# Part A's input transposed by DMA in natural token order, and read by the products with a token step of 16

## The chip, the cores and the metric

One core of a Trainium2 chip. The metric is the device time of one execution in microseconds (us); lower is better. Single executions of this kernel vary by some per cent on some chips (the kernel before took 177.28 and 177.91 us in its first rounds, 177.11 to 183.49 in those of e1), so each run carries a state (slow: more than 1.5% above the fastest run of the same kernel in its rounds; unknown: a single run), and only fast runs are compared.

In the profile, PE is TensorE's matmul stream, PEld its weight loads, DVE is VectorE, ACT is ScalarE, POOL is GpSimd, SP is the engine that issues most DMAs. The granted clock (PEclk) is the TensorE clock that the profile shows as granted, as a share of full speed. "L496" is a line of the kernel's file. The line numbers shift a little from kernel to kernel: the products that this study turns on are L496 before, L486 after, and between L486 and L498 in the experiments. They all write `u_ps`.

## The reference, cut to what matters

Part A is a linear recurrence over 2048 tokens; part B (local attention) has its own inputs and shares only the engines.

```python
dt = exp(log_dt);  Lam_bar = exp(dt * Lam)                 # complex, 448 states
Bu = einsum("bld,pd->blp", x, ((Lam_bar - 1) / Lam)[:, None] * Bmat)
h_t = Lam_bar * h_(t-1) + Bu_t                             # 2048 steps
y = 2 * einsum("blp,dp->bld", h, Cmat).real + x * Dskip
```

## The kernel before

Tokens are split into 128 chunks of 16: token = 16 p + j, with j = 4 a + b. `local(b)` computes B x for the tokens of one b, in products with 512 columns (4 values of a, 128 chunks), and adds the step from b-1. The products read x with its features on the partitions, so this kernel has TensorE transpose it, and ScalarE stores it with the 512 columns of each b side by side.

```python
def load_x(self):                       # natural rows, one DMA for each half
    self.x_sb = self.pool.tile([NCH, T, D], bf16, name="xa_sb", tag="xin")
    ...
def alloc(self):
    xa = pool.tile([KP, 4, KT, 4, NCH], bf16, name="xaT", tag="xT")   # [112, b, k, a, chunk]
    self.xT = {i: xa[:, i] for i in range(4)}
def transp(self, b, eng):               # 16 PE transposes and 2 evictions for each b
    for a in range(0, 4, 2):
        ...
                nc.tensor.transpose(pt[:, k, i, :], self.x_sb[:, 4 * (a + i) + b, k * KP:(k + 1) * KP], cx.ident[:])
        cx.ev(eng, t_[:, :, a:a + 2, :], pt[:])
def local(self, b):
    for m in range(NM):                                     # 7 blocks of states
        for k in range(KT):                                 # 4 blocks of features
            nc.tensor.matmul(ps[:], lhsT=self.Bcat[:, k, m, :],
                             rhs=self.xT[b][:, k].rearrange("p a c -> p (a c)"), ...)
        if b % 2:  ...  # + mats[1] x h[b - 1]
        if b == 3: ...  # + mats[2] x h[1]
        nc.scalar.copy(self.h[b][:, m, :], ps[:])
```

After `local` come the scan over chunks (`scan`, products `g3A`, then VectorE), corrections (`correct`) and outputs (`y`). Part B's attention sums (`pv`, written to `pvb` and `pvt`) run on VectorE beside all this. They need `vd`, some of whose rows are copied between partitions by DMA (the halo copies). The order of instructions on each engine is fixed at build time by a scheduler, not by the order of the source.

Of the kernel before, what the change touches and what calls it, by code (L numbers as in the profile page):

```python
# [10 lines left out]
ACT = mybir.ActivationFunctionType  # L11
ALU = mybir.AluOpType
f32 = mybir.dt.float32
bf16 = mybir.dt.bfloat16

S = 2048
D = 448
T = 16
NCH = 128
KT = 4  # L20
KP = 112
# [8 lines left out]
NW = 32  # L30
NM = 7
PL = 64
MA = 4
TWO_PI = 2.0 * math.pi
MAGIC = 12582912.0
# [52 lines left out]
class PartB:  # L88
# [64 lines left out]
    def transp(self, n, eng):  # L153
        nc, cx = self.nc, self.cx
        pt = cx.ps([KP, KT, 2, NCH], bf16, "pt_x", "pt")
        for i in range(2):
            for k in range(KT):
                nc.tensor.transpose(pt[:, k, i, :], self.x_sb[:, n + i, k * KP:(k + 1) * KP], cx.ident[:])
        cx.ev(eng, self.xT[:, :, n * NCH:(n + 2) * NCH], pt[:].rearrange("p k i c -> p k (i c)"))
# [115 lines left out]
class PartA:  # L275
# [7 lines left out]
    def load_params(self):  # L283
        nc, pool = self.nc, self.pool
        self.prow = pool.tile([3 * NM, 2, PL], bf16, name="prow")
        self.drow = pool.tile([KT, KP], bf16, name="drow")
        for i, src in enumerate((self.A_logdt, self.A_Lre, self.A_Lim)):
            v = src.rearrange("(m p) -> m p", p=PL).unsqueeze(1).to_broadcast([NM, 2, PL])
            nc.scalar.dma_start(self.prow[i * NM:(i + 1) * NM], v)
        nc.scalar.dma_start(self.drow[:], self.A_Dskip.rearrange("(k p) -> k p", p=KP))  # L290

    def load_bc(self):
        nc, pool = self.nc, self.pool
# [7 lines left out]
                nc.sync.dma_start(self.cn[:, a, :, ri, :], v[:, a])  # L301

    def load_x(self):
        self.x_sb = self.pool.tile([NCH, T, D], bf16, name="xa_sb", tag="xin")
        xv = self.A_x[0].rearrange("(p j) d -> p j d", j=T)
        for g in range(2):
            self.nc.sync.dma_start(self.x_sb[:, 8 * g:8 * g + 8, :], xv[:, 8 * g:8 * g + 8, :])

    def consts(self):
        nc, pool = self.nc, self.pool  # L310
# [7 lines left out]
    def params(self):  # L318
        nc, pool, V = self.nc, self.pool, self.nc.vector
        ident = self.cx.ident  # L320

        def sm(name, shape=(NCH, NM), tag=None):
            return pool.tile(list(shape), f32, name=name, tag=tag or name)

        pt = self.cx.ps([NCH, 3 * NM], bf16, "pt_p", "lg")
# [3 lines left out]
        ll = sm("ll", (NCH, 2, NM))  # L329
        V.tensor_copy(ll[:].rearrange("p r m -> p (r m)"), pt[:, NM:3 * NM])  # L330
        lre, lim = ll[:, 0], ll[:, 1]
        ptd = self.cx.ps([KP, KT], bf16, "pt_d", "lg")
        nc.tensor.transpose(ptd[:], self.drow[:], ident[0:KT, 0:KT])
        dsk = sm("dsk", (KP, KT))
        V.tensor_copy(dsk[:], ptd[:])
        kv = pool.tile([NCH, NPW, NM], f32, name="kv")
        for i, kk in enumerate(KPOW):
# [60 lines left out]
    def params_g(self):  # L398
        nc, G, ident = self.nc, self.nc.vector, self.cx.ident
        lre, lim, rden, Scat, dsk = self.lre, self.lim, self.rden, self.Scat, self.dsk  # L400
        la_re, la_im = self.pw_re[:, 0, :], self.pw_im[:, 0, :]

        def sm(name):
            return self.pool.tile([NCH, NM], f32, name=name)

        lm1, g_re, g_im, t1 = (sm(n) for n in ("lm1", "g_re", "g_im", "t1"))
        G.tensor_scalar(lm1[:], la_re, -1.0, None, op0=ALU.add)
        G.tensor_tensor(g_re[:], lm1[:], lre, op=ALU.mult)
        G.tensor_tensor(t1[:], la_im, lim, op=ALU.mult)
        G.tensor_tensor(g_re[:], g_re[:], t1[:], op=ALU.add)  # L410
        G.tensor_tensor(g_re[:], g_re[:], rden[:], op=ALU.mult)
        G.tensor_tensor(g_im[:], la_im, lre, op=ALU.mult)
        G.tensor_tensor(t1[:], lm1[:], lim, op=ALU.mult)
        G.tensor_tensor(g_im[:], t1[:], g_im[:], op=ALU.subtract)
        G.tensor_tensor(g_im[:], g_im[:], rden[:], op=ALU.mult)
        self.mat("g", self.rot_rows("Sg", g_re, g_im)[:], G)
        self.Dg = self.pool.tile([KP, KT, KP], bf16, name="Dg")
        for k in range(KT):
            nc.scalar.activation(self.Dg[:, k, :], ident[0:KP, 0:KP], ACT.Copy, scale=dsk[:, k:k + 1])

    def params_m(self):
        for i in range(NPW):
# [21 lines left out]

    def setup_b(self, engs):
        nc, cx, pool = self.nc, self.cx, self.pool
        self.Bcat = pool.tile([KP, KT, NM, NCH], bf16, name="Bcat")
        for i in range(NM):
            pt = cx.ps([KP, KT, NCH], f32, "pt_b", "pt")
            for k in range(KT):  # L450
                nc.tensor.matmul(pt[:, k, :], lhsT=self.bX[:, i, k * KP:(k + 1) * KP], rhs=self.mats["g"][:, i, :],
                                 start=(k == 0), stop=(k == KT - 1), skip_group_check=True)
            cx.ev(engs[i % len(engs)], self.Bcat[:, :, i, :], pt[:])
            yield

    def setup_c(self, engs):
        nc, cx, pool = self.nc, self.cx, self.pool
# [9 lines left out]
            yield  # L467

    def alloc(self):
        pool = self.pool  # L470
        xa = pool.tile([KP, 4, KT, 4, NCH], bf16, name="xaT", tag="xT")
        self.xT = {i: xa[:, i] for i in range(4)}
        u01 = pool.tile([NCH, 2, NM, 4 * NCH], bf16, name="u01", tag="q")
        self.h = [u01[:, 0], u01[:, 1], None, None]

    def transp(self, b, eng):
        nc, cx = self.nc, self.cx
        t_ = self.xT[b]
        for a in range(0, 4, 2):
            pt = cx.ps([KP, KT, 2, NCH], bf16, "pt_x", "pt")  # L480
            for i in range(2):
                for k in range(KT):
                    nc.tensor.transpose(pt[:, k, i, :], self.x_sb[:, 4 * (a + i) + b, k * KP:(k + 1) * KP],
                                        cx.ident[:])
            cx.ev(eng, t_[:, :, a:a + 2, :], pt[:])
            yield  # L486

    def local(self, b):
        nc, cx = self.nc, self.cx
        if b == 2:  # L490
            u23 = self.pool.tile([NCH, 2, NM, 4 * NCH], bf16, name="u23", tag="xin")
            self.h[2], self.h[3] = u23[:, 0], u23[:, 1]
        for m in range(NM):
            ps = cx.ps([NCH, 4 * NCH], f32, "u_ps", "mm")
            for k in range(KT):
                nc.tensor.matmul(ps[:], lhsT=self.Bcat[:, k, m, :], rhs=self.xT[b][:, k].rearrange("p a c -> p (a c)"),  # L496
                                 start=(k == 0), stop=(b % 2 == 0 and k == KT - 1))
            if b % 2:  # L498
                nc.tensor.matmul(ps[:], lhsT=self.mats[1][:, m, :], rhs=self.h[b - 1][:, m, :], start=False,
                                 stop=(b == 1))  # L500
            if b == 3:
                nc.tensor.matmul(ps[:], lhsT=self.mats[2][:, m, :], rhs=self.h[1][:, m, :], start=False, stop=True)  # L502
            nc.scalar.copy(self.h[b][:, m, :], ps[:])  # L503
            yield

    def _regs(self, nm):
# [92 lines left out]
    def y(self, a, b):  # L599
        nc, cx, pool = self.nc, self.cx, self.pool  # L600
        j = 4 * a + b
        ps = cx.ps([NCH, D], f32, "y_ps", "mm")
        for k in range(KT):
            nc.tensor.matmul(ps[:, k * KP:(k + 1) * KP], lhsT=self.xT[b][:, k, a, :], rhs=self.Dg[:, k, :],  # L604
                             start=(k == 0), stop=False, skip_group_check=True)
        for m in range(NM):
            nc.tensor.matmul(ps[:], lhsT=self.state(m, a, b), rhs=self.C[:, m, :], start=False, stop=(m == NM - 1),  # L607
                             skip_group_check=True)
        ya = pool.tile([NCH, D], bf16, name="ya", tag="ya", bufs=2)
        nc.scalar.copy(ya[:], ps[:])  # L610
        nc.sync.dma_start(self.out_a[:, j, :], ya[:])
# [3 lines left out]
def body(ctx: ExitStack, tc: tile.TileContext, A_x, A_Lre, A_Lim, A_Bre, A_Bim, A_Cre, A_Cim, A_logdt, A_Dskip,  # L615
         B_x, B_wqkv, B_wo, out):
    nc = tc.nc
    pool = ctx.enter_context(tc.tile_pool(name="sb", bufs=1))
    psum = ctx.enter_context(tc.tile_pool(name="ps", bufs=1, space=bass.MemoryType.PSUM))
    out_v = out[0].rearrange("(p j) e -> p j e", j=T)  # L620
    cx = Ctx(tc, pool, psum)
    b = PartB(cx, B_x, B_wqkv, B_wo, out_v[:, :, D:2 * D])
    a = PartA(cx, A_x, A_Lre, A_Lim, A_Bre, A_Bim, A_Cre, A_Cim, A_logdt, A_Dskip, out_v[:, :, 0:D])
# [38 lines left out]
    def weave(main, fill, k=1):  # L662
        for _ in main:
            for _ in range(k):
                next(fill, None)
        for _ in fill:
            pass
# [10 lines left out]
    a.params_m()  # L678
    b.norm()
    a.alloc()  # L680
    for _ in a.transp(0, "A"):
        pass
    weave(a.local(0), chain(a.transp(1, "A"), a.transp(2, "A")))
    weave(a.local(1), chain(a.transp(3, "A"), a.setup_c("A")))
    for b_ in (2, 3):
        for _ in a.local(b_):
            pass
    a.scan()
# [3 lines left out]
    for a_ in range(4):  # L692
        a.y(a_, 3)
    for b_ in (1, 0, 2):
        for _ in a.correct(b_, "A"):
            pass
        if b_ == 1:
            b.pv(4, 8)
        if b_ == 0:
            b.pv(8, 12)  # L700
        for a_ in range(4):
            a.y(a_, b_)
# [32 lines left out]
```

## Time and profile before

| | before |
|---|---|
| time | 177.59 us, median of 2 runs (177.28 to 177.91) |
| PE / DVE / ACT busy | 91% / 76% / 62% of 175.3 us |
| `u_ps` products | 112, started 216 to 217 ns apart |
| first `u_ps` product, scan's first VectorE operation | 78.84 us, 114.78 us |

The page of the kernel before: span, busy time by engine, the span in 40 slices (busy tenths, and the granted TensorE clock in tenths), then a group of instructions (busy time, mean ns of one, idle time before them and what ended it).

```profile
span 175.3 us, 2965 instructions
PE 159.6 (91%) x1171; PEld 90.8 (52%) x1175; DVE 132.6 (76%) x189; ACT 108.9 (62%) x183; POOL 5.6 (3%) x37
...
PE   7589798799799999999999999969999999999981
DVE  1299998999996894039999999999999999900000
PEclk9999999999999999999999999999999999999999
...
L496 PE MATMUL u_ps<-xaT,Bcat 112*128 112x512 bf16 x112 | 27.4, 379 | 0.1
```

A matmul's listed duration (379 ns) is longer than its spacing (216 to 217 ns): in the profile the matmuls overlap. What a product costs the stream is the distance between starts, which the timeline gives. The timeline of PE, and one line of DVE (start us, us in all, engine, line, operation):

```profile
78.84 1.24 PE L496 MATMUL u_ps<-xaT,Bcat 112*128 112x512 bf16 x5
96.55 7.07 PE L496 MATMUL u_ps<-xaT,Bcat 112*128 112x512 bf16 x32
103.68 0.38 PE L502 MATMUL u_ps<-u,mat 128*128 128x512 bf16 x1
111.47 0.38 PE L502 MATMUL u_ps<-u,mat 128*128 128x512 bf16 x1
114.78 0.68 DVE L531 TENSOR_TENSOR pc<-g3A,cosE 128x512 bf16<-128x512 f32 x1
```

The 32 products from 96.55 to 103.68 us, with the one contiguous product of another line that the trace lacks among them, are (103.68 - 96.55) / 33 = 216 ns apart; other stretches give 217, which is used below. The last product of `local` starts at 111.47 us, and scan's VectorE work at 114.78 us.

The table of windows (each column: busy us and number of instructions; at the end the granted clock, the DMA share and GB/s) shows that PE and DVE are both full in this stage:

```profile
core 0: us, PE busy (x) PEld busy (x) DVE busy (x) ACT busy (x) POOL busy (x), PEclk, DMA share, GB/s
...
83.00:96.50 13.50, 13.39 (x101) 7.70 (x102) 13.50 (x14) 12.33 (x19) 0.00 (x0) 1.00 0.01 1
96.50:111.70 15.20, 15.14 (x71) 6.83 (x71) 15.20 (x16) 8.20 (x14) 0.00 (x0) 1.00 0.01 1
```

Weight loads by shape in the kernel before (mean ns of one after the busy time):

```profile
L177 PEld LDWEIGHTS <-xbT 112*128 112x128 bf16 x64 | 8.8, 146 | 4.0 <-issue 1.3 <-PE lg L196 0.4
L604 PEld LDWEIGHTS <-xaT 112*128 112x128 bf16 x64 | 4.7, 97 | 2.7 <-issue 0.2
...
L229 PEld LDWEIGHTS <-e_all 128*128 128x128 bf16 x16 | 1.5, 146 | 0.4
```

L177 and L229 load 128 columns that are 16 elements apart, L604 adjacent ones: 146 against 97 ns.

### The profile page before, as it was taken

To read this page: it belongs to the slowest core of one execution; us is meant where nothing else is said; L and a number is where in the kernel's file an instruction comes from. 1 tells how busy PE (TensorE), PEld (TensorE's weight loads), DVE (VectorE), ACT (ScalarE), POOL (GpSimd) and SP (SyncE) were. 2 spreads that over 40 slices of the span, in tenths; PEclk is the share of its full clock that TensorE was granted. 3 is DMA by queue.
4 is the path that set the end of the run, shared out by engine and by line. 5 is a ranking of instruction groups with operands and counts; after the bars stand their busy time and mean duration, and the time that the engine had idled before them with its cause. 6 is when DMAs were issued, how large, how long until landed. Compare 5 with 4: busy or idle time off the path is not lost.

```text
span 175.3 us, 2965 instructions
## 1 busy us (share of the span) xinstructions
PE 159.6 (91%) x1171; PEld 90.8 (52%) x1175; DVE 132.6 (76%) x189; ACT 108.9 (62%) x183; POOL 5.6 (3%) x37
## 2 busy tenths in 40 slices
PE   7589798799799999999999999969999999999981
PEld 4355333445444766676565444746755455554550
DVE  1299998999996894039999999999999999900000
ACT  2279444775744876788899654356238739738382
POOL 8400000000000000000000000000000000000000
PEclk9999999999999999999999999999999999999999
DMA  5999851000370004170000000002111230140113
GB/s 155 291 297 179 90 119 30 0 4 0 87 332 0 6 0 109 50 200 8 0 4 0 0 0 0 4 0 77 33 52 52 79 108 26 52 132 30 52 54 105
DMA packets 16589, 12.36 MB, mean 70 GB/s; under 512 B 7219, under 2 KB 16065, under 8 KB 16575
## 3 DMA queue, kind: packets, MB, share of 16 engines
q1 hardware_dynamic: 16504, 12.16, 26.2%
q8 instruction: 9, 0.15, 0.4%
q14 instruction: 5, 0.04, 0.1%
q10 hardware_dynamic: 71, 0.01, 0.0%
HBM read 6.89 MB, written 3.67 MB: 60 GB/s over the span
## 4 chain that ended last, share of the span: by engine, by line
PE 51%; DVE 32%; ACT 10%; DMA 3%; issue 1%; ACTq 1%
PE y_ps L607 11%; PE qk_ps L165 11%; DVE pvb L252 9%; DVE pvt L249 8%; PE v_ps L177 7%; PE wo_ps L269 5%; PE lg L196 5%; DVE pr L192 4%; DMA drow<-in_A_Dskip_dram 3%; PE co L577 2%; ACT u L588 2%; DVE pvb L249 2%; PE y_ps L604 2%; ACT oT L264 2%; PE gt L566 1%
## 5 line engine op out<-in xcount | busy, mean ns | idle before, releaser
L192 DVE TENSOR_TENSOR pr<-qT,kT 112x2048 bf16<-112x2048 bf16 x32 | 37.0, 1219 | 0.5 <-ACT qT L77 0.5
L165 PE MATMUL qk_ps<-xbT,wqkv_nat 112*112 112x512 bf16 x128 | 32.3, 386 | 1.4 <-ACT xbT L77 1.1
L252 DVE TENSOR_TENSOR pvb<-pvb,pvt 128x1792 bf16<-128x1792 bf16 x28 | 30.3, 1083 | 0.0
L249 DVE TENSOR_TENSOR pvt<-attn,vd 128x1792 bf16<-128x1792 bf16 x28 | 30.0, 1083 | 0.0
L496 PE MATMUL u_ps<-xaT,Bcat 112*128 112x512 bf16 x112 | 27.4, 379 | 0.1
L503 ACT CAST u<-u_ps 128x512 bf16<-128x512 f32 x28 | 16.5, 590 | 9.2 <-PE u_ps L502 5.0
L165 PEld LDWEIGHTS <-wqkv_nat 112*112 112x112 bf16 x128 | 14.9, 129 | 14.1 <-issue 6.9
L607 PE MATMUL y_ps<-C,u 128*128 128x448 bf16 x84 | 18.0, 352 | 0.0
L610 ACT CAST ya<-y_ps 128x448 bf16<-128x448 f32 x16 | 8.5, 533 | 15.1 <-PE y_ps L607 14.2
L496 PEld LDWEIGHTS <-Bcat 112*128 112x128 bf16 x112 | 10.5, 97 | 10.8 <-issue 0.2
L269 PE MATMUL wo_ps<-wo_p,oT 112*128 112x448 bf16 x64 | 14.3, 353 | 1.0 <-ACT oT L264 0.9
L196 PE MATMUL lg<-pr,onesW 112*32 112x512 bf16 x128 | 12.8, 387 | 1.1 <-DVE pr L192 1.1
L177 PE MATMUL v_ps<-wqkv_nat,xbT 112*128 112x448 bf16 x64 | 13.7, 357 | 0.0
L77 ACT CAST kT<-qk_ps 112x512 bf16<-112x512 f32 x14 | 8.2, 584 | 8.1 <-PE qk_ps L165 8.1
L77 ACT CAST qT<-qk_ps 112x512 bf16<-112x512 f32 x14 | 8.2, 584 | 6.7 <-PE qk_ps L165 6.7
L271 ACT CAST yb<-wo_ps 128x448 bf16<-128x448 f32 x16 | 8.6, 539 | 5.8 <-PE wo_ps L269 5.6
L77 ACT CAST vd<-v_ps 128x448 bf16<-128x448 f32 x16 | 8.5, 533 | 4.5 <-PE v_ps L177 4.3
L177 PEld LDWEIGHTS <-xbT 112*128 112x128 bf16 x64 | 8.8, 146 | 4.0 <-issue 1.3
L210 DVE TENSOR_REDUCE mx<-pt_m 128x64 bf16<-128x512 bf16 x4 | 2.7, 687 | 10.5 <-PE pt_m L209 10.5
L588 ACT CAST u<-co 128x512 bf16<-128x512 f32 x21 | 10.6, 629 | 0.0
L607 PEld LDWEIGHTS <-u 128*128 128x128 bf16 x84 | 7.6, 97 | 5.5
L264 ACT COPY oT<-pt_o 112x1024 bf16<-112x1024 bf16 x8 | 8.1, 1047 | 2.5 <-PE pt_o L262 2.5
(175 smaller groups left out, 218.5 us busy)
## 6 DMA issues: line engine op xcount, KB each, us to landing
xb_sb<-in_B_x_dram SPq DMA_DIRECT2D x4, 448.0 KB, 7.0
xa_sb<-in_A_x_dram SPq DMA_DIRECT2D x2, 896.0 KB, 6.4
out_dram<-yb SPq DMA_DIRECT2D x8, 224.0 KB, 2.1
out_dram<-ya SPq DMA_DIRECT2D x16, 112.0 KB, 1.7
wqkv_nat<-in_B_wqkv_dram SPq DMA_DIRECT2D x3, 392.0 KB, 6.4
vd<-vd SPq DMA_DIRECT2D x1, 784.0 KB, 5.3
vd<-vd SPq DMA_DIRECT2D x1, 588.0 KB, 4.3
bX<-in_A_B_re_dram SPq DMA_DIRECT2D x1, 392.0 KB
```

The costliest lines, as they stand in the source:

```text
L77: nc.scalar.copy(out, in_)
L165: nc.tensor.matmul(ps[:], lhsT=self.wn[:, k, which, g * KP:(g + 1) * KP], rhs=self.xT[:, k, c * CH:(c + 1) * CH], start=(k == 0), stop=(k ...
L177: nc.tensor.matmul(ps[:], lhsT=xv[:, k, j, :], rhs=self.wn[:, k, 2, :], start=(k == 0), stop=(k == KT - 1))
L192: V.tensor_tensor(pr[:], self.qT[:, :, c * CH:(c + 1) * CH], self.kT[:, :, k0:k0 + CH], op=ALU.mult)
L196: nc.tensor.matmul(lg[NW * g:NW * (g + 1), :], lhsT=self.onesW[:, NW - 4 - 4 * w:2 * NW - 4 - 4 * w], rhs=pr[:, g, :], start=(w == 0), sto ...
L249: V.tensor_tensor(t_[:, 0:n], self.at[:, w, j0:j1, :].unsqueeze(2).to_broadcast([NCH, n, DH, H]), self.vd[:, off:off + n], op=ALU.mult)
L252: V.tensor_tensor(acc[:, 0:n], acc[:, 0:n], t_[:, 0:n], op=ALU.add)
L269: nc.tensor.matmul(ps[:], lhsT=oT[:, kt, i, :], rhs=self.wo_p[:, kt, :], start=(kt == 0), stop=(kt == KT - 1))
L496: nc.tensor.matmul(ps[:], lhsT=self.Bcat[:, k, m, :], rhs=self.xT[b][:, k].rearrange("p a c -> p (a c)"), start=(k == 0), stop=(b % 2 == 0 ...
L503: nc.scalar.copy(self.h[b][:, m, :], ps[:])
L588: nc.scalar.copy(h_, ps[:])
L607: nc.tensor.matmul(ps[:], lhsT=self.state(m, a, b), rhs=self.C[:, m, :], start=False, stop=(m == NM - 1), skip_group_check=True)
```

## The change

It wants to take the 64 transposes from PE and their 8 evictions from ACT, by two DMA transposes that run while part B computes. The DMA writes tokens in natural order; the products then take every sixteenth token. The kernel transposes blocks of 128 columns, so the 448 features are cut at 0, 128, 256 and 320, with the 64 doubled rows of Bcat set to zero. The correction of group 2 also moves from ACT and its identity products to VectorE. Core of the diff:

```diff
+KOFF = [0, NCH, 2 * NCH, D - NCH]
     def load_x(self):
-        self.x_sb = self.pool.tile([NCH, T, D], bf16, name="xa_sb", tag="xin")
-        xv = self.A_x[0].rearrange("(p j) d -> p j d", j=T)
-        for g in range(2):
-            self.nc.sync.dma_start(self.x_sb[:, 8 * g:8 * g + 8, :], xv[:, 8 * g:8 * g + 8, :])
+        xa = self.pool.tile([NCH, KT, S], bf16, name="xaT", tag="xin")
+        xv = xa[:].rearrange("d k (p a b) -> d b k a p", a=4, b=4)
+        self.xT = [xv[:, b] for b in range(4)]
+        for k in (3, slice(0, 3)):
+            c0, c1 = (D - NCH, D) if k == 3 else (0, 3 * NCH)
+            self.nc.sync.dma_start_transpose(out=xa[:, k, :], in_=self.A_x[0][:, c0:c1])
 ...
+        nc.gpsimd.memset(self.Bcat[0:PL, 3], 0.0)
 ...
-    def transp(self, b, eng):            # (all of it)
 ...
-                nc.tensor.matmul(ps[:], lhsT=self.Bcat[:, k, m, :], rhs=self.xT[b][:, k].rearrange("p a c -> p (a c)"),
+                nc.tensor.matmul(ps4[:], lhsT=self.Bcat[:, k, m, :], rhs=self.xT[b][:, k],
 ...
-    for _ in a.transp(0, "A"):
-        pass
-    weave(a.local(0), chain(a.transp(1, "A"), a.transp(2, "A")))
-    weave(a.local(1), chain(a.transp(3, "A"), a.setup_c("A")))
-    for b_ in (2, 3):
+    weave(a.local(0), a.setup_c("A"))
+    for b_ in (1, 2, 3):
 ...
-        for _ in a.correct(b_, "A"):
+        for _ in a.correct(b_, "V" if b_ == 2 else "A"):
```

More of the change, by code (lines that the diff above doesn't have):

```diff
@@ L285, in load_params @@
         self.prow = pool.tile([3 * NM, 2, PL], bf16, name="prow")
-        self.drow = pool.tile([KT, KP], bf16, name="drow")
+        self.drow = pool.tile([KT, NCH], bf16, name="drow")
         for i, src in enumerate((self.A_logdt, self.A_Lre, self.A_Lim)):
@@ L289, in load_params @@
             nc.scalar.dma_start(self.prow[i * NM:(i + 1) * NM], v)
-        nc.scalar.dma_start(self.drow[:], self.A_Dskip.rearrange("(k p) -> k p", p=KP))
+        nc.scalar.dma_start(self.drow[0:3, :], self.A_Dskip[0:3 * NCH].rearrange("(k p) -> k p", p=NCH))
+        nc.scalar.dma_start(self.drow[3:4, :], self.A_Dskip[D - NCH:D].unsqueeze(0))
     def load_bc(self):
@@ L331, in params @@
         lre, lim = ll[:, 0], ll[:, 1]
-        ptd = self.cx.ps([KP, KT], bf16, "pt_d", "lg")
+        ptd = self.cx.ps([NCH, KT], bf16, "pt_d", "lg")
         nc.tensor.transpose(ptd[:], self.drow[:], ident[0:KT, 0:KT])
-        dsk = sm("dsk", (KP, KT))
+        dsk = sm("dsk", (NCH, KT))
         V.tensor_copy(dsk[:], ptd[:])
@@ L416, in params_g @@
         self.mat("g", self.rot_rows("Sg", g_re, g_im)[:], G)
-        self.Dg = self.pool.tile([KP, KT, KP], bf16, name="Dg")
+        self.Dg = self.pool.tile([NCH, KT, NCH], bf16, name="Dg")
         for k in range(KT):
-            nc.scalar.activation(self.Dg[:, k, :], ident[0:KP, 0:KP], ACT.Copy, scale=dsk[:, k:k + 1])
+            nc.scalar.activation(self.Dg[:, k, :], ident[:], ACT.Copy, scale=dsk[:, k:k + 1])
     def params_m(self):
@@ L446, in setup_b @@
         nc, cx, pool = self.nc, self.cx, self.pool
-        self.Bcat = pool.tile([KP, KT, NM, NCH], bf16, name="Bcat")
+        self.Bcat = pool.tile([NCH, KT, NM, NCH], bf16, name="Bcat")
         for i in range(NM):
-            pt = cx.ps([KP, KT, NCH], f32, "pt_b", "pt")
+            pt = cx.ps([NCH, KT, NCH], f32, "pt_b", "pt")
             for k in range(KT):
-                nc.tensor.matmul(pt[:, k, :], lhsT=self.bX[:, i, k * KP:(k + 1) * KP], rhs=self.mats["g"][:, i, :],
+                d0 = KOFF[k]
+                nc.tensor.matmul(pt[:, k, :], lhsT=self.bX[:, i, d0:d0 + NCH], rhs=self.mats["g"][:, i, :],
                                  start=(k == 0), stop=(k == KT - 1), skip_group_check=True)
@@ L469, in alloc @@
     def alloc(self):
-        pool = self.pool
-        xa = pool.tile([KP, 4, KT, 4, NCH], bf16, name="xaT", tag="xT")
-        self.xT = {i: xa[:, i] for i in range(4)}
-        u01 = pool.tile([NCH, 2, NM, 4 * NCH], bf16, name="u01", tag="q")
-        self.h = [u01[:, 0], u01[:, 1], None, None]
-    def transp(self, b, eng):
-        nc, cx = self.nc, self.cx
-        t_ = self.xT[b]
-        for a in range(0, 4, 2):
-            pt = cx.ps([KP, KT, 2, NCH], bf16, "pt_x", "pt")
-            for i in range(2):
-                for k in range(KT):
-                    nc.tensor.transpose(pt[:, k, i, :], self.x_sb[:, 4 * (a + i) + b, k * KP:(k + 1) * KP],
-                                        cx.ident[:])
-            cx.ev(eng, t_[:, :, a:a + 2, :], pt[:])
-            yield
+        u01 = self.pool.tile([NCH, 2, NM, 4 * NCH], bf16, name="u01", tag="q")
@@ L488, in local @@
+        u23 = self.pool.tile([NCH, 2, NM, 4 * NCH], bf16, name="u23", tag="xT")
+        self.h = [u01[:, 0], u01[:, 1], u23[:, 0], u23[:, 1]]
     def local(self, b):
         nc, cx = self.nc, self.cx
-        if b == 2:
-            u23 = self.pool.tile([NCH, 2, NM, 4 * NCH], bf16, name="u23", tag="xin")
-            self.h[2], self.h[3] = u23[:, 0], u23[:, 1]
         for m in range(NM):
-            ps = cx.ps([NCH, 4 * NCH], f32, "u_ps", "mm")
+            ps4 = cx.ps([NCH, 4, NCH], f32, "u_ps", "mm")
+            ps = ps4[:].rearrange("p a c -> p (a c)")
@@ L495, in local @@
             for k in range(KT):
-                nc.tensor.matmul(ps[:], lhsT=self.Bcat[:, k, m, :], rhs=self.xT[b][:, k].rearrange("p a c -> p (a c)"),
+                nc.tensor.matmul(ps4[:], lhsT=self.Bcat[:, k, m, :], rhs=self.xT[b][:, k],
                                  start=(k == 0), stop=(b % 2 == 0 and k == KT - 1))
             if b % 2:
-                nc.tensor.matmul(ps[:], lhsT=self.mats[1][:, m, :], rhs=self.h[b - 1][:, m, :], start=False,
+                nc.tensor.matmul(ps, lhsT=self.mats[1][:, m, :], rhs=self.h[b - 1][:, m, :], start=False,
@@ L500, in local @@
                                  stop=(b == 1))
             if b == 3:
-                nc.tensor.matmul(ps[:], lhsT=self.mats[2][:, m, :], rhs=self.h[1][:, m, :], start=False, stop=True)
-            nc.scalar.copy(self.h[b][:, m, :], ps[:])
+                nc.tensor.matmul(ps, lhsT=self.mats[2][:, m, :], rhs=self.h[1][:, m, :], start=False, stop=True)
+            nc.scalar.copy(self.h[b][:, m, :], ps)
             yield
@@ L603, in y @@
         for k in range(KT):
-            nc.tensor.matmul(ps[:, k * KP:(k + 1) * KP], lhsT=self.xT[b][:, k, a, :], rhs=self.Dg[:, k, :],
+            c0 = PL if k == 3 else 0
+            d0 = KOFF[k] + c0
+            nc.tensor.matmul(ps[:, d0:KOFF[k] + NCH], lhsT=self.xT[b][:, k, a, :], rhs=self.Dg[:, k, c0:],
                              start=(k == 0), stop=False, skip_group_check=True)
```

## The prediction

> **What bounds the kernel now.** The page gives PE 91% of 175.3 us, DVE 76%, ACT 62%. By stage (table of windows): from 83 to 111.7 us PE is busy 28.5 of 28.7 us and DVE 28.7; from 126 to 168 us PE is busy 41.3 of 42, while DVE stops at 153 us. The chain of waits names DVE from 78 to 121 us, but those are attention products (pv) that could run at any time; the recurrence (scan), which everything after needs, waits for PE to finish `local` at 111.7 us. So PE work between 75 and 112 us, and in the tail, is worth its time nearly one for one.
>
> **Removed.** 64 PE transposes of A's x: blocks of 8 in about 0.44 us on the timeline, 3.5 us of PE. With them go 8 ACT evictions at 1.02 us and the wait at the start: the first `u_ps` product starts at 78.84 us, behind two transpose blocks and their evictions. I expect the end of `local` 4 to 5 us earlier. In the tail, correct(2) loses 7 identity products (217 ns pitch, 1.5 us of PE) and 7 ACT evictions.
>
> **Added or moved.**
> - Two DMA transposes, 2.1 MB. The old load was issued at 45.7 us, when B's x buffer came free, and landed 6.4 us later; that gate stays. [...] No such transfer is in this trace.
> - correct(2) on DVE: 7 additions of 128x512 from PSUM at about 0.6 us (as scan's `pc`), where DVE is idle. Free if the build-time order does not put them ahead of the last pv.
> - 64 skip products (L604) get weights at stride 16. The strided loads already here (xbT, e_all) show 146 ns against 97 contiguous, and a pitch near 72 ns where the contiguous L604 has 50: plus 1.5 us.
> - 112 `u_ps` products read 512 moving columns 32 bytes apart: the open term. [...] no moving operand in this trace is strided, so the size is not shown. If a moving column costs what a strided weight column seems to (63 ns per 128, estimated), a 512 product goes from 217 to about 250 ns: plus 4 us, which eats the gain. If it halves the rate: plus 24 us, some 20 visible.
>
> **Sum.** No stride penalty: 177.6 - 4.5 - 1.5 + 1.5 = about 173. Small penalty: 177. Half rate: about 195. I hold the first most likely, since strided weight loads disturb the stream by only about 10 ns each (V products 199 ns pitch against 190 for Part A's y).
>
> Predicted 174.0 us, 80% range 170 to 196. Chances: faster by over 2% 0.43, within 2% 0.24, slower by over 2% 0.33.
>
> **What would show it.** Right: `u_ps` products still 217 ns apart on the timeline; `local` over at 107 us; the transposes landed before 75 us; PE busy down 4 to 5 us. Wrong: `u_ps` spaced 250 ns or more, `local` ending after 112 us, DVE idle before the scan; or PE idle at 76 us with the DMA transpose as releaser; or the last pv held behind correct(2) on DVE, seen as DVE idle around 140 to 155 us.
>
> **What would make it wrong.** Above all the moving stride; second, transposes that take over 30 us or hold back the halo copies of `vd` queued behind them at 67 us; third, another instruction order from the scheduler.

177.6 - 4.5 - 1.5 + 1.5 is 173.1; with 4 us for a small penalty it is 177, with the 24 us of half rate, some 20 of them visible, about 195. The forecast, 174.0, lies near the first. The 63 ns for 128 strided weight columns are an estimate; the trace shows 63 ns as the pitch of the products of L229, whose weights are strided (three from 79.92 to 80.11 us).

## The result, and the profile after

The changed kernel took 256.85 us, median of 2 runs (255.42 to 258.28), against 177.59. The ratio is 1.446 (95% interval 1.410 to 1.483). Here and below a ratio is the mean time of one kernel's fast runs over that of the other's in the same rounds, so not quite the ratio of the medians. (In e1 and e12 the ratio fits only without the first of the four runs; with all fast runs it would be 0.974 and 1.040.)

The same parts of the page after the change:

```profile
span 253.3 us, 2815 instructions
PE 239.5 (95%) x1102; PEld 94.2 (37%) x1104; DVE 136.8 (54%) x196; ACT 98.7 (39%) x168; POOL 6.5 (3%) x38
...
PE   7779889899999999999999999999999799999994
DVE  0799999969600539999100000000005999999710
PEclk9999999999998555555555555555557999999999
...
L486 PE MATMUL u_ps<-xaT,Bcat 128*128 128x512 bf16 x112 | 106.5, 1098 | 0.2 <-issue 0.2
L521 DVE TENSOR_TENSOR pc<-g3A,cosE 128x512 bf16<-128x512 f32 x1 | 0.7, 693 | 71.8 <-PE g3A L519 71.8
```

The span grew by 78.0 us, and PE's busy time by 79.9. One group holds it: L486, the `u_ps` products, now 1098 ns long instead of 379. The granted clock falls to 5 tenths from slice 14 to slice 30, although PE is shown as busy nearly all the time. The second group says that VectorE then sat idle for 71.8 us before the scan's first operation.

The timeline after (PE, and at the end the line of DVE):

```profile
75.25 3.83 PE L486 MATMUL u_ps<-xaT,Bcat 128*128 128x512 bf16 x4
...
94.21 14.87 PE L486 MATMUL u_ps<-xaT,Bcat 128*128 128x512 bf16 x16
...
112.98 0.61 PE L489 MATMUL u_ps<-u,mat 128*128 128x512 bf16 x1
...
192.88 0.69 DVE L521 TENSOR_TENSOR pc<-g3A,cosE 128x512 bf16<-128x512 f32 x1 [71.78 <-PE g3A L519]
```

From the first start to the last, 15 steps in 14.87 - 1.10 = 13.77 us: the products are 918 ns apart, 4.2 times as far as before. L489, the contiguous product of the same size, takes 400 ns (112.98 to 113.38 us) instead of 217, at a granted clock of 0.50. DVE's scan work starts at 192.88 us, 78.1 us later than before; from there to the end it takes 60.4 us after and 60.5 us before. So the whole loss lies ahead of the scan.

The table of windows after:

```profile
core 0: us, PE busy (x) PEld busy (x) DVE busy (x) ACT busy (x) POOL busy (x), PEclk, DMA share, GB/s
45.40:54.00 8.60, 8.08 (x50) 3.34 (x51) 8.60 (x10) 4.17 (x7) 0.00 (x0) 1.00 0.93 197
...
75.20:78.90 3.70, 3.70 (x8) 0.50 (x6) 0.99 (x2) 0.53 (x1) 0.00 (x0) 1.00 0.85 242
...
109.10:133.70 24.60, 24.40 (x30) 3.93 (x30) 12.00 (x12) 3.51 (x6) 0.00 (x0) 0.50 0.00 1
```

Two things are read here. First, at 75.2 to 78.9 us the clock is still 1.00, and the four products of that stretch (3.83 us) are already (3.83 - 1.10) / 3 = 910 ns apart. The slow products came before the slow clock. Second, while the DMA transposes ran (45.4 to 54 us) the core moved 197 GB/s; they had landed by 56 us (second issue at 47.7 us, 8.4 us to landing), 19 us before their first use.

The sum, as an estimate from these numbers: 112 products at 918 - 217 ns are +78.5 us; 21 contiguous products at half clock +3.8; other small products at half clock about +2. Against that, the start came 3.6 us earlier (75.25 instead of 78.84), about 2.2 us of transposes within `local` (five blocks of 0.45 us) are gone, and the scan no longer waits about 2 us behind a pv sum. That gives about +76.5 of the 78.1 measured; the rest is not accounted for.

### The profile page after: what moved, and what is told of

It is laid out like the page before. It is cut to its first block, busy times and chain, and to the rows that moved or that the text cites. A ratio compares the mean times of both kernels' runs of the same rounds, so it can differ in the third digit from the quotient of the medians.

```text
span 253.3 us, 2815 instructions
## 1 busy us (share of the span) xinstructions
PE 239.5 (95%) x1102; PEld 94.2 (37%) x1104; DVE 136.8 (54%) x196; ACT 98.7 (39%) x168; POOL 6.5 (3%) x38
## 4 chain that ended last, share of the span: by engine, by line
PE 78%; DVE 12%; ACT 5%; DMA 2%; issue 1%; ACTq 1%
PE u_ps L486 40%; PE y_ps L599 8%; PE qk_ps L166 7%; PE v_ps L178 5%; PE wo_ps L270 4%; PE lg L197 4%; DVE pr L193 3%; ACT u L578 3%; PE u_ps L489 2%; DMA drow<-in_A_Dskip_dram 2%; PE y_ps L596 1%; PE u_ps L492 1%; ACT oT L265 1%; PE gt L556 1%; PE pt_c L470 1%; DVE gsc L530 1%
## 5 line engine op out<-in xcount | busy, mean ns | idle before, releaser
L486 PE MATMUL u_ps<-xaT,Bcat 128*128 128x512 bf16 x112 | 106.5, 1098 | 0.2 <-issue 0.2
L486 PEld LDWEIGHTS <-Bcat 128*128 128x128 bf16 x112 | 14.4, 131 | 68.2 <-issue 68.2
L521 DVE TENSOR_TENSOR pc<-g3A,cosE 128x512 bf16<-128x512 f32 x1 | 0.7, 693 | 71.8 <-PE g3A L519 71.8
L250 DVE TENSOR_TENSOR pvt<-attn,vd 128x1792 bf16<-128x1792 bf16 x28 | 30.3, 1097 | 0.0
L270 PE MATMUL wo_ps<-wo_p,oT 112*128 112x448 bf16 x64 | 13.6, 353 | 0.4 <-ACT oT L265 0.2
L232 DVE RECIPROCAL rec<-tp 128x48 f32<-128x48 f32 (+1 forms) x6 | 2.4, 420 | 12.9 <-PE tp L230 12.9
```

What stands on the lines that cost most here:

```text
L250: V.tensor_tensor(t_[:, 0:n], self.at[:, w, j0:j1, :].unsqueeze(2).to_broadcast([NCH, n, DH, H]), self.vd[:, off:off + n], op=ALU.mult)
L270: nc.tensor.matmul(ps[:], lhsT=oT[:, kt, i, :], rhs=self.wo_p[:, kt, :], start=(kt == 0), stop=(kt == KT - 1))
L486: nc.tensor.matmul(ps4[:], lhsT=self.Bcat[:, k, m, :], rhs=self.xT[b][:, k], start=(k == 0), stop=(b % 2 == 0 and k == KT - 1))
```

## Experiments

My theory after seeing the result: a moving operand whose columns lie 32 bytes apart costs TensorE 1.79 ns a column (918 / 512). The rivals: the DMA transposes themselves; the clock as a cause of its own; any step other than 1; the distance rather than the 16-byte line. That 16 bytes are the grain was my supposition: no run had shown it yet, and e2 and e9 test it.

A note on correctness: all runs were judged correct, even those which read wrong tokens. The recurrence changes part A's output by at most 0.0006 where the skip term reaches 0.021, so that judgement hardly sees it. In a simulation the root mean square error of part A against the reference is 0.29% for the kernels before and after and for the runs e7, e13 and e15 below, and 6.9% for e1, which reads wrong tokens.

### e1: the same kernel with adjacent columns

```diff
-                nc.tensor.matmul(ps4[:], lhsT=self.Bcat[:, k, m, :], rhs=self.xT[b][:, k],
+                nc.tensor.matmul(ps, lhsT=self.Bcat[:, k, m, :], rhs=self.xa[:, k, 512 * b:512 * b + 512],
```

> The changed kernel in everything, but the 112 input products read 512 adjacent tokens instead of 512 tokens 16 apart (wrong tokens on purpose, so a wrong result is expected). Stride theory: the u_ps products come back to about 217 ns apart, the granted clock to 1.0, and the kernel takes 170 to 174 us, a little under before (177.6). Rival, the DMA transposes: if what they wrote or how they ran is the cause, the u_ps products stay near 919 ns apart and the time near 257 us. Rival, the clock: if the clock drop were a thing of its own, it would stay near 0.5 in this stage and the products near 430 ns apart.

The result was 174.59 us (median of 4, one of them slow), ratio 0.972 to before (0.953 to 0.991). The products in the view of the tile `u_ps` (min, median and max duration, first and last start):

```profile
L487 PE MATMUL u_ps<-xaT,Bcat x110: 377/379/381, 77.8 to 108.9; 128*128 128x512 bf16 x110
```

They have their 379 ns again. The DMA transposes and everything else of the change are still in, so they are not the cause. With the step gone the clock stays up as well (mean 0.988 in the profiled run, 0.778 in that of the change), so its fall was not a thing of its own.

### e3: the stride without the DMA transposes

```diff
-        xa = pool.tile([KP, 4, KT, 4, NCH], bf16, name="xaT", tag="xT")
-        self.xT = {i: xa[:, i] for i in range(4)}
+        xa = pool.tile([KP, KT, S], bf16, name="xaT", tag="xT")
+        xv = xa[:].rearrange("d k (p a b) -> d b k a p", a=4, b=4)
+        self.xT = [xv[:, b] for b in range(4)]
```

> The kernel before with its TensorE transposes, but the transposed x is stored in natural token order, so that the products read with a step of 16 as in the change; no DMA transpose. Right result. Stride theory: u_ps products 919 ns apart, clock near 0.5 in the stage, about 260 us in all. If the DMA transposes are needed for the loss: about 178 us.

One run, 270.35 us. The same view:

```profile
L498 PE MATMUL u_ps<-xaT,Bcat x112: 1075/1097/1105, 85.8 to 203.1; 112*128 112x512 bf16 x112
```

PE transposes, no DMA transpose, and the products are at 1097 ns once more. So the step brings the slow products without any DMA transpose. The run is over the 260 us expected, and much of that is a second cost of the step that I had overlooked: ScalarE now stores the transposed columns 32 bytes apart, and each of the 8 evictions takes 4.59 us instead of 1.02. On the page of this run:

```profile
L77 ACT COPY xaT<-pt_x 112x1024 bf16<-112x1024 bf16 x8 | 36.2, 4590 | 0.7 <-PE pt_x L484 0.7
```

The first product waits 2.68 us for one of them and starts at 85.81 us, 7.0 us later than in the kernel before. The run's mean granted clock was 0.764, and three products of L229 among the slow ones were (90.72 - 90.38) / 3 = 113 ns apart instead of the (80.11 - 79.92) / 3 = 63 of the kernel before. So this run alone does not part the step from the clock; the 910 ns at a clock of 1.00 in the changed kernel do, and e2 does it again.

### e2: a ladder of steps

```diff
+        self.xs = [xa[:].rearrange("d k (c s) -> d k s c", s=s)[:, :, 0:n, 0:512 // n]
+                   for s, n in ((2, 1), (4, 1), (8, 2), (32, 8))]
-                                 rhs=self.xT[b][:, k],
+                                 rhs=self.xs[b][:, k],
```

> The changed kernel, but the four groups of input products read with a step of 2, 4, 8 and 32 elements (4, 8, 16 and 64 bytes) instead of 16 elements in all four (wrong tokens on purpose). Theory of the 16-byte lines[...]: steps 2 and 4 near 217 ns apart, 8 slow, 32 as slow as 16 (919 ns). Rival, any step other than 1 is slow by the same factor: all four groups near 919 ns. Rival, cost grows with the distance: 8 clearly faster than 919 ns and 32 clearly slower.

One run, 221.43 us. The PE timeline: step 4 (four products up to the next line), then 28 products at step 8 with the first four at step 32, then step 32 alone.

```profile
88.69 1.96 PE L489 MATMUL u_ps<-xaT,Bcat 128*128 128x512 bf16 x4
90.47 0.40 PE L492 MATMUL u_ps<-u,mat 128*128 128x512 bf16 x1
...
100.81 28.79 PE L489 MATMUL u_ps<-xaT,Bcat 128*128 128x512 bf16 x32
129.42 0.60 PE L492 MATMUL u_ps<-u,mat 128*128 128x512 bf16 x1
...
130.25 3.62 PE L489 MATMUL u_ps<-xaT,Bcat 128*128 128x512 bf16 x4
133.68 0.60 PE L492 MATMUL u_ps<-u,mat 128*128 128x512 bf16 x1
```

Step 4: (90.47 - 88.69) / 4 = 445 ns. Step 32: (133.68 - 130.25) / 4 = 858 ns. Step 8: (129.42 - 100.81 - 4 x 0.858) / 28 = 899 ns. Step 2, from a mixed stretch at 84 us, about 226 ns. Steps 2 and 4 ran at a granted clock of 1.00 and step 32 at 0.50. Step 8 ran at both: 5 products from 100.8 to 104.4 us at 1.00, and 14 from 107.1 to 118.8 us at 0.50, each time 900 ns apart. As in the changed kernel (910 ns at 1.00, 918 at 0.50), the slow products do not follow the clock; in both runs the clock falls only 4 to 5 us after they begin (75.25 to about 80 us in the changed kernel, 100.8 to about 105.5 us here). So neither rival holds: not every step is slow (step 2 took 226 ns), and distance does not count beyond 16 bytes (899, 918 and 858 ns at steps 8, 16 and 32). But my own expectation failed as well. Two reads in each line (step 4) are not free; they cost double (445 ns).

### e9: lines, not steps

The pattern in e2 suggested a cost for each 16-byte line touched. This run tests it with patterns in which lines, steps and jumps come apart.

```diff
-        self.xs = [xa[:].rearrange("d k (c s) -> d k s c", s=s)[:, :, 0:n, 0:512 // n]
-                   for s, n in ((2, 1), (4, 1), (8, 2), (32, 8))]
+        g16, g8 = (xa[:].rearrange("d k (c s) -> d k c s", s=s) for s in (16, 8))
+        g3 = xa[:, :, 0:1536].rearrange("d k (c s) -> d k s c", s=3)
+        self.xs = [g16[:, :, :, 0:4], g3[:, :, 0, :], g8[:, :, :, 0:2], g16[:, :, 0:64, 4:12]]
```

> Wrong tokens on purpose, other patterns for the four groups. Line theory: a product of 512 columns takes the longer of 217 ns and 1.79 ns times the number of 16-byte lines that it touches. 4 adjacent of every 16 elements (128 lines): 217 to 232 ns, as step 2 (226 ns). Step 3 (192 lines): about 344 ns. 2 adjacent of every 8 elements (256 lines): about 459 ns, although every line is hit twice. 8 adjacent of every 16 that straddle a line boundary (128 lines): 217 to 232 ns. Rival, the cost is of jumps in the address pattern and not of lines: 4 of 16 and 8 of 16 would differ (128 and 64 jumps) and 2 of 8 would be like neither. Rival, two hits per line are enough: 2 of 8 stays near 217 ns.

One run, 182.62 us; the clock was 1.00 throughout the stage. The PE timeline: step 3, then 28 products with 2 of every 8, with the first four products of the last kind and a missing contiguous one, then 8 of every 16:

```profile
87.61 1.52 PE L491 MATMUL u_ps<-xaT,Bcat 128*128 128x512 bf16 x4
88.96 0.38 PE L494 MATMUL u_ps<-u,mat 128*128 128x512 bf16 x1
...
97.06 13.70 PE L491 MATMUL u_ps<-xaT,Bcat 128*128 128x512 bf16 x32
110.81 0.38 PE L497 MATMUL u_ps<-u,mat 128*128 128x512 bf16 x1
...
111.03 1.06 PE L491 MATMUL u_ps<-xaT,Bcat 128*128 128x512 bf16 x4
111.93 0.38 PE L494 MATMUL u_ps<-u,mat 128*128 128x512 bf16 x1
```

| pattern (512 columns) | lines | expected ns | measured ns | ns for each line |
|---|---|---|---|---|
| adjacent | 64 | 217 | 217 | hidden |
| step 2 (e2) | 128 | 217 to 232 | 226 | 1.77 |
| 4 of every 16 (12 steps from 83.3 us) | 128 | 217 to 232 | 228 | 1.78 |
| 8 of every 16, across a line's edge | 128 | 217 to 232 | 225 | 1.76 |
| step 3 | 192 | 344 | (88.96 - 87.61) / 4 = 338 | 1.76 |
| 2 of every 8 | 256 | 459 | (110.81 - 97.06 - 4 x 0.225 - 0.217) / 28 = 451 | 1.76 |
| step 4 (e2) | 256 | - | 445 | 1.74 |
| step 8 (e2) | 512 | - | 899 | 1.76 |
| step 16 (the change) | 512 | - | 918 | 1.79 |
| step 32 (e2) | 512 | - | 858 | 1.68 |

The theory holds for every pattern: a product takes the longer of 217 ns and some 1.76 ns for each 16-byte line. The rivals fail: with a cost for each jump, step 3 (512 jumps) would be as dear as step 16, and it took 338 ns; with two hits enough, 2 of every 8 would take 217, and it took 451. The last row is a little low, and I did not follow that up.

### e7: two neighbours of each line, in a right kernel

```diff
-                nc.tensor.matmul(ps4[:], lhsT=self.Bcat[:, k, m, :], rhs=self.xT[b][:, k],
+                nc.tensor.matmul(ps4[:].rearrange("p a c -> p c a"), lhsT=self.Bcat[:, k, m, :],
+                                 rhs=self.xT[b][:, k].rearrange("d a p -> d p a"),
```

> The changed kernel with the same bytes read in another order: chunk outside, the four tokens of a group inside, so that two neighbouring reads share a 16-byte line (256 lines a product instead of 512); the columns are put back in order by the PSUM address of the output. Right result. Line theory: about 450 ns a product, half of 919, and about 203 us. If writing PSUM out of order costs more than that, the products are slower than 450 ns; if only the innermost step counted and not the lines, 446 ns too, as step 4 was.

One run, 198.65 us. Four products up to the next line:

```profile
94.66 1.96 PE L486 MATMUL u_ps<-xaT,Bcat 128*128 128x512 bf16 x4
96.44 0.40 PE L490 MATMUL u_ps<-u,mat 128*128 128x512 bf16 x1
```

(96.44 - 94.66) / 4 = 445 ns: the same bytes in another order at half the cost, and some 58 us under the change (256.85 us) for a swap of two loops. The scattered PSUM writes showed no cost of their own; one hidden behind the 445 ns of the reads would not show. The clock stayed at 1.00 in the whole stage (columns as in the tables of windows above):

```profile
76.00:134.00 58.00, 57.34 (x185) 18.36 (x188) 32.60 (x41) 20.64 (x35) 0.00 (x0) 1.00 0.06 16
```

So at 445 ns the clock did not fall, and at 858 to 918 ns (e2 and the change) it did.

### e5: the reordering done by the DMA

A contiguous operand needs the tokens sorted by b. Here the DMA does it, with 32 transposes of 128 rows each.

```diff
-        xa = self.pool.tile([NCH, KT, S], bf16, name="xaT", tag="xin")
+        xa = self.pool.tile([NCH, 4, KT, 4, NCH], bf16, name="xaT", tag="xin")
+        self.xT = [xa[:, b] for b in range(4)]
+        xr = self.A_x[0].rearrange("(p j) d -> j p d", j=T)
+        for b in range(4):
+            for a in range(4):
+                self.nc.sync.dma_start_transpose(out=xa[:, b, 3, a, :], in_=xr[4 * a + b][:, D - NCH:D])
+                self.nc.sync.dma_start_transpose(out=xa[:, b, 0:3, a, :], in_=xr[4 * a + b][:, 0:3 * NCH])
```

> The changed kernel with the reordering moved into the DMA: 32 transposes of 128 tokens each, whose source rows are 16 tokens apart, write x in the order in which the products read it, contiguous. Right result. Stride theory: u_ps 217 ns apart, about 171 to 174 us, faster than before by 2 to 3 per cent, if the transposes land by 75 us (issued from 45 us on, 8.6 us of issue for the two large ones[...]). If small transposes cost over 1 us each in issue, they land after 78 us and PE waits for them with the transpose as releaser, and the time is 177 us or more.

It took 182.16 us (median of 4), ratio 1.022 (1.012 to 1.033): slower than before, though the products were 217 ns apart and `local` ended at 107 us. The issue queue on SP, first and last transpose and the first halo copy:

```profile
45.58 1.20 SPq L311 DMA_TRANSPOSE xaT<-in_A_x_dram  x1
...
86.53 1.25 SPq L312 DMA_TRANSPOSE xaT<-in_A_x_dram  x1
87.89 0.61 SPq L182 DMA_DIRECT2D vd<-vd  x1
```

And of VectorE in the same run:

```profile
92.78 2.09 DVE L250 TENSOR_TENSOR pvt<-attn,vd 128x1792 bf16<-128x1792 bf16 x2 [9.21 <-DMA vd<-vd]
```

Each transpose holds the queue for about 1.25 us, whether 128 or 384 columns wide (mostly 1.23 and 1.25), so 32 of them fill it from 45.6 to 87.8 us. PE did not have to wait, as I had feared, because the transposes of b = 0 come first (its first product started at 75.42 us). The victim was another: the halo copies of `vd`, issued at 66.8 us in the changed kernel, came at 87.9 us, and VectorE waited 9.2 us for them. The scan's first operation came at 118.84 us (110.39 in e13 below); PE waited 10.2 us for it, and the mean granted clock of the profiled run was 0.971.

### e8 and e12: the second half after the halo copies, by source order

```diff
-    a.load_x()
+    a.load_x(0, 2)
     weave(b.qk(3), vproj(), 4)
+    a.load_x(2, 4)
```

> As the permuted DMA transposes, but only the 16 transposes of the first half (b = 0 and 1) are issued before the halo copies of vd; the 16 of the second half are issued after them. Queue theory: what the permuted version lost is the halo copies waiting in the issue queue behind 32 transposes of 1.25 us each (DVE waited 9.2 us for vd). Then here that wait is gone, the scan starts at about 111 us, and the kernel takes 171 to 174 us, 2 to 4 per cent under before. If the transposes slow other work in another way, it stays at 178 us or more. Risk: the last 8 transposes land at about 99 us, just when b = 3 needs them.

> The same with the correction of group 2 back on ScalarE with its identity products, as in the kernel before. If the moved correction is worth the 1.5 us of TensorE that I put down for it, this is 1 to 2 us slower than the split version with the correction on VectorE; if the tail is bound elsewhere, the same within 0.5 us.

e8 took 185.23 us (ratio 1.037, 1.027 to 1.047), e12 185.96 us (1.046, 1.033 to 1.059). The edit did not do what it says. In e8's trace the halo copies were issued at 91.4 us, behind all 32 transposes: the built order did not follow the source. Why is argued only: the scheduler seems to sort the queue by what is ready. So e8 neither supports nor hurts the queue theory. e12 against e8 (intervals overlap) settles nothing about the moved correction.

### e13: the same with an order edge

```diff
-    a.load_x(2, 4)
+    with tc.issue_after(b.last_halo.ins):        # the last halo copy: order in the queue, no wait for its end
+        a.load_x(2, 4)
```

> The split version once more, with an order edge this time, since the scheduler had put all 32 transposes ahead of the halo copies again (the copies were issued at 91 us in that run). The build now has the 16 transposes of the first half, the halo copies, then the other 16. Queue theory: halo copies at 67 and 75 us as before, no DVE wait for vd, scan near 111 us, and 171 to 174 us (2 to 4 per cent under the kernel before); the last transposes are issued by 97 us, so PE may wait up to 2 us at b = 3. If DVE still waits some 10 us for vd, or the time stays above 178 us, the queue was not the cause.

The issue queue, and one line of PE:

```profile
65.78 1.25 SPq L318 DMA_TRANSPOSE xaT<-in_A_x_dram  x1
67.13 0.61 SPq L182 DMA_DIRECT2D vd<-vd  x1
...
74.53 0.54 SPq L182 DMA_DIRECT2D vd<-vd  x1
...
75.98 2.72 SPq L317 DMA_TRANSPOSE xaT<-in_A_x_dram  x1
...
100.22 1.04 PE L493 MATMUL u_ps<-xaT,Bcat 128*128 128x512 bf16 x4 [1.92 <-DMA xaT<-in_A_x_dram]
```

The halo copies are back at 67 and 75 us, and the VectorE wait for `vd` is gone. The four fast runs took 172.45, 172.47, 173.05 and 174.67 us; of the four runs of the kernel before in these rounds only one was fast (177.15 us), so there is no interval. The queue theory holds: with the copies in time, the wait and some 9 us are gone against e5. PE waits 1.92 us for the last transposes at b = 3, as expected.

### e15: four of them in the gap

SP idles between 68.6 and 74.5 us. Four transposes of b = 2 go there.

```diff
-    with tc.issue_after(b.last_halo.ins):
-        a.load_x(2, 4)
+    with tc.issue_after(b.halos[0].ins):
+        a.load_b(2, 3, (0, 1))
+    with tc.issue_after(b.halos[1].ins):
+        a.load_b(2, 3, (2, 3))
+        a.load_b(3, 4)
```

> The version with the second half after the halo copies left PE waiting 1.9 us for the last transposes at b = 3, while the issuing queue sat idle from 69 to 74 us between the two pairs of halo copies. Here 4 of the second 16 transposes (5 us of issue) go into that gap. Expected: the wait at b = 3 is gone, the scan starts about 1.5 to 2 us earlier than 110.4 us unless VectorE is still in a pv sum, and the time is 1 to 2 us under the version before it (172.5 us in its fast runs), 3 to 4 per cent under the kernel before. If VectorE or the tail holds it, the same 172.5 us.

The median was 171.73 us of 7 runs, ratio 0.968 (0.964 to 0.972). This beats both kernels: 3.2% under before and a third under the change. The wait at b = 3 is gone. The gain over e13's fast runs is about 1 us by the medians, at the lower end of what I expected; it is across different chips, so it is not shown.

### e4 and e14: the moved correction alone

The kernel before with only `"V" if b_ == 2 else "A"`, twice.

> The kernel before with only the correction of group 2 moved to VectorE: 1 to 1.5 us faster than before if the 7 identity products are on the chain; the same if not. Slower only if the last pv sums are put behind it on VectorE.

> The kernel before with the correction of group 2 on VectorE, repeated for a narrower interval and a profile in the fast state: 1 to 2 per cent under before. If the first result was chance: within 0.5 per cent of before.

e4: 175.71 us (median of 4), ratio 0.984 (0.973 to 0.994). e14: fast runs of 174.73, 175.52 and 175.72 us against one fast run of before, 177.15. So about 1 to 1.6% of the 3.2% in e15 is the correction, as far as these runs can tell, and the rest is the transposes, if the two simply add.

## Why the prediction was wrong

I predicted 174.0 us with a range up to 196; the result was 256.85.

- **The step that failed: "I hold the first most likely, since strided weight loads disturb the stream by only about 10 ns each", and the sizes given to the open term.** I named the moving operand's stride as the first risk, but no trace gave its size, and I sized it three ways, 0, +4 and +24 us. It measured 112 x (918 - 217) ns = +78.5 us, over three times my worst case, and my range ended at half rate, where the runs show a quarter (918 ns against 217).
- **The proxy.** I took 63 ns for 128 weight columns to be what 128 moving columns would cost; they cost 128 x 1.79 = 229 ns. Why the weight loads did not warn of this is not shown. One possible reason: 63 ns is also the pitch of the products of L229 (three in 0.19 us from 79.92 us), and at their 144 columns they would take 144 x 217 / 512 = 61 ns with no stride at all, an estimate from the 217 ns of 512 columns. Then the 63 ns never measured a stride.
- **Second effects that I had not listed.** Among the slow products the clock fell to half, and 21 contiguous ones took nearly twice as long (400 ns at 0.50 instead of 217); in e2 and the change it fell at a spacing of 858 to 918 ns, in e7 at 445 it did not. The busy share that the trace shows does not tell the clock: PE was 99% busy at 0.50 (24.40 of 24.60 us from 109.1 us, after) and at 1.00 (13.39 of 13.50 us from 83 us, before). DVE idled 71.8 us, since its build-time order has the scan ahead of the last pv sums; I had listed that as a sign ("DVE idle before the scan"). The time from the scan to the end did not grow, so the trace shows no cost of that idling by itself.
- **Right:** PE's work ahead of the scan is worth its time one for one (PE +79.9 us busy, span +78.0, scan to end 60.4 against 60.5 us). The transposes landed in time, by 56 us, well within the 75 us needed; the core moved 197 GB/s while they ran. The rate that I had taken for them came from no trace. Without the stride the rest came to 174.59 us in e1, against my "about 173", with a wide interval.
- **Mis-sized:** the strided skip weights. I put +1.5 us; the group of four takes 0.22 us after (203.80 to 204.02 us) against 0.20 before (126.00 to 126.20), +0.02 x 16 = 0.3 us. The pitch near 72 ns that I compared with 50 can only be that of L229, whose products have 144 columns where those of L604 have 112; by an estimate from these, 50 x 144 / 112 = 64 of the 72 is width.
- **The queue risk** ("hold back the halo copies of `vd` queued behind them") did not strike the change, whose transposes are issued in 8.6 us, but it struck e5 for 9.2 us.

## What to carry to other kernels

Before a moving operand is read with a step, count the distinct 16-byte lines of one product: above some 123 lines for 512 columns (217 / 1.76, an estimate) it costs about 1.76 ns a line here, and with one 2-byte column in each line that is four times the contiguous product (899 and 918 ns at steps 8 and 16, against 217). A strided store costs as well (e3: 4.59 us an eviction instead of 1.02). If a stride cannot be avoided, order the columns so that neighbours share a line (e7: 445 ns instead of 918 for swapping two loops), or let the transfer sort the data (e13, e15). When many DMAs are added to a queue, look at what is queued behind them, and check the built order: source order did not hold in e8, an order edge did in e13.
